# One kernel, three edits in its front: a stated engine order up to the first width transform, folds in three steps a group, and one-hot rows four chunks at a time

## The chip, the cores and the metric

The kernel runs on one core of a Trainium2 chip. The metric is device time in microseconds, the median of several executions. A core has TensorE (PE; its weight loads are PEld), VectorE (DVE), ScalarE (ACT), GpSimd (POOL), and SyncE (SP), which here only issues DMAs. Each engine has its own queue of instructions; semaphores order the engines among each other.

## The reference

Three steps, of float32 arrays; x is 8 x 3072 x 256:

```python
X = np.fft.fft(x, axis=1); X = np.fft.fft(X, axis=2); x = X.real.reshape(24576, 256)
# then, over the rows in order: 8 experts, capacity 768
expert = argmax(x @ w_gate); gate = softmax(x @ w_gate)[expert]
# the first 768 rows of each expert are kept; all other rows of the output are zero
y = relu(x_kept @ w1[e]) @ w2[e]              # 256 -> 1024 -> 256
out = gate * y
# then for every row
h = out @ w_in; out = maximum(0.01 * h, h) @ w_out   # 256 -> 2048 -> 256
```

Since at most 8 x 768 rows are not zero, the kernel transforms only the batches in which the experts fill up: two whole ones and half of a third (NSTAT = 3), and checks at the end that they were enough.

## The kernel before

Everything that needs float32 precision on TensorE is split into a high and a low part (`split`: ACT copies the high part, VectorE subtracts it from the source, which gives the low part, the residue), and a product is three matmuls (`mm3`, lines 199 to 201: high x low parts of both sides).

For each batch the work has four stages.

- **Fold** (`fold_steps`): x comes in three chunks of 128 x 8 x 256 (`xj`, 1 MB, two buffers, loaded by SP in `next_x`). VectorE folds the eight symmetric rows and two halves of columns into sums and differences: `a0` makes `fe` (sums), differences in place, and `q` (differences of differences, also in place, in the second half of x); `a1` works on `fe`, `b0` on `q`; both write `raw`. `a0` ends with the load of the next chunk. A stated list gives the order of the nine steps.
- **S1**, the transform over the sequence: `raw` is split to `fh` and `fl` (`fsplit_j`, for batch 0 by chunk; `fsplit_steps` for the others, by pairs of classes), and multiplied by the tables `th`, `tl`. Batch 0 runs S1 chunk by chunk (`s1_first`: all eight accumulators stay open, and `group(j)` adds chunk j); the others run class by class (`s1_steps`). The accumulators are evacuated to `pch`, `pcl`, `psh`, `psl` by ACT and VectorE (`s1_ev_odd`, `s1_ev_even`).
- **S2**, the transform over the width, with the gate's eight columns beside it (`s2_steps`): 12 chunks of 128 rows, 14 matmuls each in batches 0 and 1 (7 in batch 2), into `psu`; ACT evacuates to `yd`, `ym`, sends them to memory and copies the logits to L. The matmul of line 643 adds the special rows: `spec` times the small table `smov`.
- **Routing** (`route`): `one`, `mm`, `two` find each row's expert and place; then `put`: for each of 25 chunks, `hot` builds two one-hot rows on VectorE (`oha`, `ohr`: lines 819 and 820) and `place` multiplies them on TensorE, which writes row numbers into the slot table (`tab`, `self.slots`). From the table `prep` (GpSimd) gathers the experts' rows.

Ahead of batch 0's S2 stand also: the tables, loaded in six halves through staging tiles that share the room of `pch` to `psl` (`load_table`); the width tables `mv..` (`build_tables`); the gate's columns and `smov` (`build_gate`); the column of x that has no partner (`special_fold`, `special`, whose result is `spec`).

After the routing of two batches the experts start (`moe_static`), TensorE-heavy, with the other weights' conversion as background; then the last two products.

What sets the order: the program emits instructions in one order; a scheduler reorders them by its own model of time, on all engines but SP, which keeps the emission order (`in_order("SP")`, line 1443). Background steps wait in a list `bg` with a cost each; `step` emits a foreground step, adds its credit, and emits background steps as far as the credit goes; `upto` empties the list. Lines 1196 to 1241 emit the front.

Of the kernel before, what the change touches and what calls it, by code (L numbers as in the profile page):

```python
# [8 lines left out]
F32 = mybir.dt.float32  # L9
# [134 lines left out]
class Kern:  # L144
# [91 lines left out]
    def build_tables(self, tmp, yp, nb):  # L236
# [11 lines left out]
        nc.sync.dma_start(out=sk, in_=a[f"sk{nb}"])  # L248
        self.sk = sm, sk

    def build_gate(self, tmp, nb):
        nc = self.nc
        f, ft, wg = self.b0[:3]
        mv = self.smov[nb]
        sm, sk = self.sk
        ps = self.ps2.tile([P, 512], F32, name="ps_c", tag="v")
        for i in range(2):
            for k in range(2):
                nc.tensor.matmul(out=ps[:, 8 * i:8 * i + 8], lhsT=ft[:, k, 128 * i:128 * i + 128],
                                 rhs=wg[:, k], start=k == 0, stop=k == 1)  # L260
        for k in range(2):
            nc.tensor.matmul(out=ps[:96, 16:24], lhsT=ft[:, k, 256:352], rhs=wg[:, k],
                             start=k == 0, stop=k == 1)
        for i, n in enumerate("csn"):
            hi, lo = self.mv[n + "h"], self.mv[n + "l"]
            if n == "n":
                self.act(hi[:, D:], self.mv["sh"][:, D:].bitcast(F32), scale=-1.0)
                self.act(lo[:, D:], self.mv["sl"][:, D:].bitcast(F32), scale=-1.0)
            else:
                self.split(hi[:, D:], lo[:, D:], ps[:, 8 * i:8 * i + 8])  # L270
        wh = tmp.tile([96, E], F32R, name="wh", tag="wh")
        wl = tmp.tile([96, E], F32R, name="wl", tag="wl")
        self.split(wh, wl, ps[:96, 16:24])
        self.act(mv[:, :, :D], sm)
        V = nc.vector
        for b in range(nb):
            t0 = tmp.tile([96, E], F32, name="smt0", tag="smt0")
            V.tensor_scalar(out=t0, in0=wh.bitcast(F32), scalar1=sk[:, b, 0:1], scalar2=None, op0=ALU.mult)
            t1 = tmp.tile([96, E], F32, name="smt1", tag="smt1")
            V.tensor_scalar(out=t1, in0=wl.bitcast(F32), scalar1=sk[:, b, 1:2], scalar2=None, op0=ALU.mult)  # L280
            self.tt(mv[:, b, D:], t0, t1, ALU.add)
# [47 lines left out]
    def fold_steps(self, b):  # L329


        tmp = self.tmp

        def copy(o, x):
            self.nc.vector.tensor_copy(out=o, in_=x)
        st, loc, xt, kb = [], {}, self.xt, bkey(b)
        tt = self.tt
        A, M = ALU.add, ALU.subtract

        def extra():  # L340
            xe = xt[kb, "e"]
            t = tmp.tile([1, 3 * P], F32, name="ee", tag="ee")
            c7, x4, o7 = (t[:, P * i:P * i + P] for i in range(3))
            tt(t[:, :D], xe[:, 0], xe[:, 1], A)
            tt(xe[:, 0], xe[:, 0], xe[:, 1], M)
            tt(c7, c7, x4, A)
            tt(o7, xe[:, 0, :P], xe[:, 0, P:], M)
            loc["c7"], loc["o7"], loc["x4"] = c7, o7, x4

        def fix():  # L350
            ce, r, c7 = loc["ce", 0], loc["r"], loc["c7"]
            tt(r[0:1, 4, 0], ce[0:1, 0], c7, M)
            tt(r[0:1, 5, 0], ce[0:1, 0], c7, A)
            copy(loc["x4"], ce[0:1, 1])

        def a0(j):
            x = xt[kb, j]
            if j == 0:
                extra()
            if j == 0:  # L360
                loc["r"] = self.rawp.tile([P, 8, 3, P], F32, name="raw", tag="raw")
            e = tmp.tile([P, 8, P], F32, name="fe", tag="fe")
            q = x[:, 0:4, P:]
            loc["e"], loc["o", j] = e, q
            tt(e, x[:, :, :P], x[:, :, P:], A)
            tt(x[:, :, :P], x[:, :, :P], x[:, :, P:], M)
            tt(q, x[:, 0::2, :P], x[:, 1::2, :P], M)
            self.next_x()

        def a1(j):  # L370
            e, r = loc["e"], loc["r"]
            c = e[:, 0::2]
            tt(c, c, e[:, 1::2], A)
            ce = tmp.tile([P, 2, P], F32, name="ce", tag="ce")
            loc["ce", j] = ce
            tt(ce, c[:, 0::2], c[:, 1::2], A)
            tt(r[:, 0:2, j], c[:, 0::2], c[:, 1::2], M)
            tt(r[:, 4, j], ce[:, 0], ce[:, 1], M)
            tt(r[:, 5, j], ce[:, 0], ce[:, 1], A)
            if j == 0:  # L380
                fix()

        def b0(j):
            o, r = loc["o", j], loc["r"]
            se = tmp.tile([P, 2, P], F32, name="se", tag="se")
            tt(se, o[:, 0::2], o[:, 1::2], M)
            tt(r[:, 2:4, j], o[:, 2::-2], o[:, 3::-2], A)
            tt(r[:, 6, j], se[:, 0], se[:, 1], A)
            tt(r[:, 7, j], se[:, 0], se[:, 1], M)
            if j == 0:  # L390
                copy(r[0:1, 3, 0], r[0:1, 2, 0])
                copy(r[0:1, 6, 0], se[0:1, 1])
                copy(r[0:1, 2, 0], loc["o7"])

        ca = (3.1, 2.1, 1.6)
        for f, j in ((a0, 0), (a1, 0), (a0, 1), (b0, 0), (a1, 1), (a0, 2), (b0, 1), (a1, 2), (b0, 2)):
            st.append((ca[(a0, a1, b0).index(f)], lambda f=f, j=j: f(j)))
        self.floc = loc
        return st
# [112 lines left out]
    def s1_first(self):  # L512
# [7 lines left out]
        def group(j):  # L520
            for fn, cls in (("c", 0), ("s", 2)):
                for par in "AB":
                    js = [jj for jj, _, _ in self.ODD[par]]
                    if j in js:
                        self.s1_mm(banks[fn + par][:, :384], cls, "A", j, j == js[0], j == js[-1], par)
            for cls, name, fn, r, n in self.EVEN:
                w = 386 if name == "C" else 384
                self.s1_mm(banks[name][:, :w], cls, name, j, j == 0, j == 2 and name != "C")
                if j == 2 and name == "C":
                    self.s1_extra(banks[name][:, :w])  # L530

        def evens(q):
            for e in self.EVEN[q:q + 2]:
# [88 lines left out]
    def s2_steps(self, b, L, bi, mode):  # L622
# [29 lines left out]
        for c in range(12):  # L652
# [6 lines left out]
            def go(c=c, m=m):  # L659
# [10 lines left out]
                if m == "v":  # L670
                    V = self.ps2.tile([P, 512], F32, name="psv", tag="v")
                    part(V[:, :NL], "s", "s", c, True, True)
                    vs = yp.tile([P, NL], F32, name="vs", tag="vs", bufs=1)
                    self.act(vs, V[:, :NL])
                    self.tt(yd, U[:, :NL], vs, ALU.subtract)
                    self.tt(ym, U[:, :NL], vs, ALU.add)
# [18 lines left out]
        if mirror:  # L695
            def mid():
                U = cosp("p", 12, True, 1)
                y = yp.tile([1, NR], F32, name="yx", tag="vs", bufs=1)
                self.act(y[:, :NL], U[:1, :NL])
                self.act(y[:, NL:], rt[0:1, 1, 12:13])  # L700
                nc.scalar.dma_start(out=dst(1536 + 3, 1), in_=y)
# [7 lines left out]
    def route(self, b, L, n):  # L709
# [2 lines left out]
        V, G = nc.vector, nc.gpsimd  # L712
        loc = {}
        nput = min(n, NCH - 1)

        def t3(name, dt=F32):
            return rp.tile([P, NCH, E], dt, name=name, tag=name)[:, :n]
# [89 lines left out]
                    self.act(o, t)  # L807
                loc.update(hi=hi, lo=lo)

        w = self.ntab // P  # L810
        w2 = w + w % 2

        def hot(c, m):

            a = rp.tile([P, HG, P], F32, name="oha", tag="oha", bufs=2)
            r = rp.tile([P, HG, w2], F32, name="ohr", tag="ohr", bufs=2)
            for i in range(m):
                k = slice(c + i, c + i + 1)
                V.tensor_scalar(out=a[:, i], in0=self.iota, scalar1=loc["lo"][:, k], scalar2=None, op0=ALU.is_equal)
                V.tensor_scalar(out=r[:, i], in0=self.iota[:, :w2], scalar1=loc["hi"][:, k],  # L820
                                scalar2=self.rt[:, b, 0, k], op0=ALU.is_equal, op1=ALU.mult)
            loc["h", c] = a, r

        def place(c, m):
# [338 lines left out]
    def static(self, rps):  # L1163
# [28 lines left out]
        def run(*steps):  # L1192
            for f in steps:
                f[1]() if isinstance(f, tuple) else f()

        run(fs[0], fs[1], fs[3], *tb[0])
        tb.append(self.load_table(self.pt, 2))
        self.special_load(0)
        self.load_consts()
        self.reset_routing()  # L1200
        self.load_build(self.tmp, self.yp)
        run(lambda: ready(0), fs[2], fs[4], *tb[1], fs[6], lambda: ready(1), fs[5], fs[7], fs[8], *tb[2],
            lambda: self.build_tables(self.tmp, self.yp, NSTAT), lambda: ready(2))
        self.special_fold()
        self.later(self.fold_steps(1))
        loc = self.floc
        self.new_p()
        ev = [f for _, f in evac]
        run(ev[0], ev[1], lambda: self.build_gate(self.tmp, NSTAT), ev[2], ev[3], self.special)
        pend, put0 = None, []  # L1210
        for b in range(NSTAT):
            last = b == NSTAT - 1
            if b:
# [13 lines left out]
                    self.later(fs[:1] + [(1.5, mm), (1.5, two)] + fs[1:])  # L1227
                for s in self.s1_steps():
                    self.step(*s)
            if not last:  # L1230
                self.later(self.fsplit_steps(loc))
                if b:
                    self.later(put)
            L = self.new_l()
            for s in self.s2_steps(b, L, b, (lambda c: "d") if last else
                                   (lambda c: "p")):
                self.step(*s)
            self.upto(len(put) if b and not last else 0)
            if last:
                self.full_flag()  # L1240
            pend = self.route(b, L, 12 if last else NCH)
# [109 lines left out]
    def general(self):  # L1351
        tc, nc = self.tc, self.nc
        with ExitStack() as es:
# [6 lines left out]
                    fn()  # L1360
            self.load_build(self.tmp, self.yp)
            self.build_tables(self.tmp, self.yp, 1)
            self.build_gate(self.tmp, 1)
            self.init_table()
            if not self.fast:
# [129 lines left out]
```

## Time and profile before

| | |
|---|---|
| median of 3 runs | 1030.39 us (1030.28 to 1030.99) |
| profiled execution | 1030.87 us, its span 1029.1 us |
| busy in the span | PE 951.8 (92%), PEld 903.2 (88%), DVE 636.4 (62%), ACT 481.8 (47%), POOL 126.8 (12%) |
| mean granted clock of TensorE | 0.974 of full speed |

The shares are means over the whole span; stages differ, and the rows below go by stretches.

### The profile page before, as it was taken

Reading aid. Unit: us, or ns where it says so; the run is one execution under the profiler, and the core shown is the slowest. Engines: PE = TensorE matmul, PEld = TensorE weight load, DVE = VectorE, ACT = ScalarE, POOL = GpSimd, SP = SyncE. Lnnn points to the kernel's source line nnn. Section 1 sums busy time; section 2 is a strip of 40 time slices with the busy share of each in tenths; the row PEclk is TensorE's granted clock in tenths of the full one; section 3 lists DMA queues with packets and bytes.
Section 4 is the critical chain, followed back from the end, with each engine's and each line's share of the span. In section 5 each row is a group of like instructions: output and inputs, shape, how many; then the busy total and the mean of one; then the engine's idle time right before and its main releaser. Section 6 shows DMA issues by size and latency. Waiting matters only on the chain. (4 is left out here: it accounts for less than half of the span.)

```text
span 1029.1 us, 15401 instructions
## 1 busy us (share of the span) xinstructions
PE 951.8 (92%) x5563; PEld 903.2 (88%) x5563; DVE 636.4 (62%) x1445; ACT 481.8 (47%) x1075; POOL 126.8 (12%) x178
## 2 busy tenths in 40 slices
PE   1749997989999999999999999999999999999993
PEld 1639996888999999998999999999999999999992
DVE  8997575979898635453555555555455555555551
ACT  4234631546665534453544444444444454445441
POOL 1000002063232221100001100110011100110011
PEclk9969997999999999999999999999999999999997
DMA  8324522479879655400000000000010000000000
GB/s 312 129 87 164 190 83 75 156 232 322 302 264 366 207 190 193 144 32 31 20 28 32 16 22 26 32 22 21 21 32 32 16 17 32 33 16 6 11 16 18
DMA packets 56192, 101.51 MB, mean 99 GB/s; under 512 B 5189, under 2 KB 39369, under 8 KB 54956
## 3 DMA queue, kind: packets, MB, share of 16 engines
q1 hardware_dynamic: 47000, 73.20, 21.1%
q0 software_dynamic: 4640, 12.81, 3.8%
q10 hardware_dynamic: 4468, 14.44, 3.5%
q8 instruction: 45, 0.74, 0.3%
q14 instruction: 39, 0.32, 0.1%
HBM read 54.54 MB, written 45.89 MB: 98 GB/s over the span
## 5 line engine op out<-in xcount | busy, mean ns | idle before, releaser
L185 DVE TENSOR_TENSOR gf<-gt,psg 128x384 f32<-128x384 f32 x256 | 141.8, 554 | 218.2 <-ACT gt L188 214.8
L188 ACT ACTIVATE gt<-psg 128x384 f32<-128x384 f32 x256 | 126.0, 492 | 253.7 <-PE psg L201 253.6
L1099 PE MATMUL po<-wo,gh 128*128 128x512 f32 x768 | 232.3, 394 | 0.0
L199 PE MATMUL psg<-yh,wi 128*128 128x384 f32 x512 | 172.7, 338 | 1.9 <-ACT yh L188 1.9
L200 PE MATMUL psg<-yl,wi 128*128 128x384 f32 x512 | 173.0, 338 | 0.0
L201 PE MATMUL psg<-yh,wi 128*128 128x384 f32 x512 | 172.7, 337 | 0.0
L185 DVE TENSOR_TENSOR gl<-gf,gh 128x384 fp32r<-128x384 f32 x256 | 141.4, 552 | 17.5 <-ACT gh L188 17.4
L1099 PEld LDWEIGHTS po<-wo,gh 128*128 128x128 f32 x768 | 139.8, 188 | 12.3
L1100 PE MATMUL po<-wo,gl 128*128 128x256 f32 x768 | 149.6, 281 | 0.0
L188 ACT ACTIVATE gh<-gf 128x384 fp32r<-128x384 f32 x256 | 132.8, 519 | 18.1 <-PE po L1099 17.8
L1100 PEld LDWEIGHTS po<-wo,gl 128*128 128x128 f32 x768 | 128.4, 188 | 4.0
L1110 POOL DMA_INDIRECT out<-ob,mix x48 | 46.9, 977 | 551.5 <-DVE ob L1109 477.9
L1042 DVE SCALAR_TENSOR_TENSOR hl<-psh,hh 128x384 fp32r<-128x384 f32 x128 | 70.0, 553 | 60.8 <-ACT hh L188 60.2
L199 PEld LDWEIGHTS psg<-yh,wi 128*128 128x128 f32 x512 | 96.6, 189 | 9.4 <-ACT yh L188 2.2
L200 PEld LDWEIGHTS psg<-yl,wi 128*128 128x128 f32 x512 | 96.8, 189 | 8.3
L201 PEld LDWEIGHTS psg<-yh,wi 128*128 128x128 f32 x512 | 96.5, 188 | 2.1
L199 PE MATMUL psy<-hh,w2h 128*128 128x384 f32 x256 | 87.9, 343 | 0.8 <-DVE hl L1042 0.8
L199 PE MATMUL psh<-xTh,w1h 128*128 128x384 f32 x256 | 86.8, 340 | 1.9 <-DVE hl L1042 1.3
L201 PE MATMUL psy<-hh,w2l 128*128 128x384 f32 x256 | 86.4, 338 | 0.0
L200 PE MATMUL psy<-hl,w2h 128*128 128x384 f32 x256 | 86.2, 337 | 0.0
L201 PE MATMUL psh<-xTh,w1l 128*128 128x384 f32 x256 | 86.0, 336 | 0.0
L200 PE MATMUL psh<-xTl,w1h 128*128 128x384 f32 x256 | 85.9, 336 | 0.0
(224 smaller groups left out, 1421.9 us busy)
## 6 DMA issues: line engine op xcount, KB each, us to landing
out<-zero SPq DMA_DIRECT2D x48, 512.0 KB, 8.8
xj<-in_xg SPq DMA_DIRECT2D x9, 1024.0 KB, 5.0
w1r<-in_w SPq DMA_DIRECT2D x9, 1024.0 KB, 7.9
w2r<-in_w SPq DMA_DIRECT2D x9, 1024.0 KB, 7.2
y_kept<-yf ACTq DMA_DIRECT2D x16, 384.0 KB, 6.2
yf<-y_kept SPq DMA_DIRECT2D x16, 384.0 KB, 3.0
y_first<-yd ACTq DMA_DIRECT2D x9, 530.0 KB, 2.8
w<-in_w_in SPq DMA_DIRECT2D x8, 512.0 KB, 5.2
```

What stands on the lines that cost most here:

```text
L185: self.nc.vector.tensor_tensor(out=o, in0=x, in1=y, op=op)
L188: self.nc.scalar.activation(out=o, in_=x, func=func, scale=scale)
L199: nc.tensor.matmul(out=out, lhsT=lh, rhs=rh, start=start and i == 0, stop=False)
L200: nc.tensor.matmul(out=out, lhsT=lh, rhs=rl, start=False, stop=False)
L201: nc.tensor.matmul(out=out, lhsT=ll, rhs=rh, start=False, stop=stop and i == n - 1)
L1042: nc.vector.scalar_tensor_tensor(out=lo, in0=ps[:, :T], scalar=0.0, in1=hi.bitcast(F32), op0=ALU.max, op1=ALU.subtract)
L1099: mm(out=o, lhsT=gh[:, c], rhs=both, start=f == 0, stop=False)
L1100: mm(out=o[:, :D], lhsT=gl[:, c], rhs=first, start=False, stop=f == NF2 - 1)
L1110: i = nc.gpsimd.indirect_dma_start(out=self.a["out"][0:nr], out_offset=bass.IndirectOffsetOnAxis(ap=s["ix"][:, k, 1:2], axis=0), in_=ob, i ...
```

## The change

1. The engine order of PE, DVE, ACT and POOL is stated (emission order) from the fold of batch 0 to the end of its S2; behind that point the scheduler orders again. The front's emission is rewritten: fold steps, table halves, `ready(j)`, `build_tables`, `special_fold`, `build_smov` (moved out of `build_gate`), evacuations, `build_gate`, `special`; batch 1's fold and fsplit become background steps beneath S2 of batch 0 (before, its fold was put in the list earlier, and fsplit after it). In `group(j)` the cosine classes, odd and even, go ahead of the sine classes. In `build_gate` the three copies go ahead of the three subtractions.
2. `q` gets a tile of its own (`fq`), so b0 no longer reads x; each chunk's steps go a0, a1, b0. `vs` and `yx` take tiles of the ring `ev`.
3. `hot` makes the one-hot rows of up to four chunks with three operations instead of two for each chunk.

```diff
+    def build_smov(self, nb):
+        self.act(self.smov[nb][:, :, :D], self.sk[0])
...
-        for i, n in enumerate("csn"):
-            hi, lo = self.mv[n + "h"], self.mv[n + "l"]
-            if n == "n":
-                self.act(hi[:, D:], self.mv["sh"][:, D:].bitcast(F32), scale=-1.0)
-                self.act(lo[:, D:], self.mv["sl"][:, D:].bitcast(F32), scale=-1.0)
-            else:
-                self.split(hi[:, D:], lo[:, D:], ps[:, 8 * i:8 * i + 8])
...
-        self.split(wh, wl, ps[:96, 16:24])
-        self.act(mv[:, :, :D], sm)
+        parts = [(self.mv["ch"][:, D:], self.mv["cl"][:, D:], ps[:, :8]),
+                 (self.mv["sh"][:, D:], self.mv["sl"][:, D:], ps[:, 8:16]), (wh, wl, ps[:96, 16:24])]
+        for hi, _, src in parts:
+            self.act(hi, src)
+        for hi, lo, src in parts:
+            self.tt(lo, src, hi, ALU.subtract)
+        for h in "hl":
+            self.act(self.mv["n" + h][:, D:], self.mv["s" + h][:, D:].bitcast(F32), scale=-1.0)
...
-            q = x[:, 0:4, P:]
+            q = tmp.tile([P, 4, P], F32, name="fq", tag="fq")
...
-        for f, j in ((a0, 0), (a1, 0), (a0, 1), (b0, 0), (a1, 1), (a0, 2), (b0, 1), (a1, 2), (b0, 2)):
+        for f, j in ((a0, 0), (a1, 0), (b0, 0), (a0, 1), (a1, 1), (b0, 1), (a0, 2), (a1, 2), (b0, 2)):
...
-            for cls, name, fn, r, n in self.EVEN:
-                w = 386 if name == "C" else 384
-                self.s1_mm(banks[name][:, :w], cls, name, j, j == 0, j == 2 and name != "C")
-                if j == 2 and name == "C":
-                    self.s1_extra(banks[name][:, :w])
+                for cls, name, _, r, n in [e for e in self.EVEN if e[2] == fn]:
+                    w = 386 if name == "C" else 384
+                    self.s1_mm(banks[name][:, :w], cls, name, j, j == 0, j == 2 and name != "C")
+                    if j == 2 and name == "C":
+                        self.s1_extra(banks[name][:, :w])
...
-                    vs = yp.tile([P, NL], F32, name="vs", tag="vs", bufs=1)
+                    vs = yp.tile([P, NL], F32, name="vs", tag="ev", bufs=3)
...
-                y = yp.tile([1, NR], F32, name="yx", tag="vs", bufs=1)
+                y = yp.tile([1, NR], F32, name="yx", tag="ev", bufs=3)
...
-            for i in range(m):
-                k = slice(c + i, c + i + 1)
-                V.tensor_scalar(out=a[:, i], in0=self.iota, scalar1=loc["lo"][:, k], scalar2=None, op0=ALU.is_equal)
-                V.tensor_scalar(out=r[:, i], in0=self.iota[:, :w2], scalar1=loc["hi"][:, k],
-                                scalar2=self.rt[:, b, 0, k], op0=ALU.is_equal, op1=ALU.mult)
+            o = rp.tile([P, HG, w2], F32, name="oho", tag="oho")
+            cs = slice(c, c + m)
+            at = lambda x, k: x[:, cs, None].to_broadcast([P, m, k])
+            row = lambda k: self.iota[:, None, :k].to_broadcast([P, m, k])
+            self.tt(a[:, :m], at(loc["lo"], P), row(P), ALU.is_equal)
+            self.tt(o[:, :m], at(loc["hi"], w2), row(w2), ALU.is_equal)
+            self.tt(r[:, :m], o[:, :m], at(self.rt[:, b, 0], w2), ALU.mult)
...
-        run(fs[0], fs[1], fs[3], *tb[0])
+        front = self.in_order("PE", "DVE", "Activation", "Pool")
+        front.__enter__()
+        run(fs[0], tb[0][0], fs[1], fs[2], tb[0][1])
         tb.append(self.load_table(self.pt, 2))
         self.special_load(0)
         self.load_consts()
         self.reset_routing()
         self.load_build(self.tmp, self.yp)
-        run(lambda: ready(0), fs[2], fs[4], *tb[1], fs[6], lambda: ready(1), fs[5], fs[7], fs[8], *tb[2],
-            lambda: self.build_tables(self.tmp, self.yp, NSTAT), lambda: ready(2))
+        run(lambda: ready(0), fs[3], tb[1][0], fs[4], fs[5], tb[1][1], lambda: ready(1))
+        self.build_tables(self.tmp, self.yp, NSTAT)
         self.special_fold()
-        self.later(self.fold_steps(1))
-        loc = self.floc
+        run(tb[2][0], fs[6], tb[2][1], fs[7], fs[8], lambda: ready(2))
+        self.build_smov(NSTAT)
         self.new_p()
         ev = [f for _, f in evac]
         run(ev[0], ev[1], lambda: self.build_gate(self.tmp, NSTAT), ev[2], ev[3], self.special)
+        fs, loc = self.fold_steps(1), self.floc
+        split = self.fsplit_steps(loc)
+        self.later(fs[:2] + split[:1] + fs[2:] + split[1:])
...
-            if not last:
-                self.later(self.fsplit_steps(loc))
-                if b:
-                    self.later(put)
+            if b and not last:
+                self.later(self.fsplit_steps(loc) + put)
...
             self.upto(len(put) if b and not last else 0)
+            if not b:
+                front.__exit__(None, None, None)
```

## Rows read from the trace of the kernel before

**Rows 1.** Busy time by stretch: bounds, length, engines (instructions), granted clock, DMA share, GB/s

```profile
52.40:67.90 15.50, 0.45 (x3) 0.19 (x2) 15.28 (x40) 5.80 (x13) 0.00 (x0) 0.63 0.25 76
67.90:92.00 24.10, 24.10 (x175) 23.95 (x176) 21.10 (x53) 11.58 (x37) 0.00 (x0) 0.88 0.46 178
92.00:129.20 37.20, 37.20 (x264) 35.27 (x263) 21.55 (x67) 20.30 (x60) 0.33 (x3) 1.00 0.45 163
...
220.00:1015.00 795.00, 786.02 (x4511) 748.27 (x4509) 463.99 (x934) 392.48 (x855) 99.89 (x118) 1.00 0.25 86
```

**Rows 2.** Waits of TensorE in the first 240 us: total, times, longest

```profile
PE psu L643 <- ACT fh L188: 15.1, 1, 15.1
```

**Rows 3.** Timeline of TensorE: start, length, instruction, what ended its idle time

```profile
52.43 0.41 PE L617 MATMUL ps<-altn,th 1*96 1x386 f32 x1
67.90 0.56 PE L643 MATMUL psu<-smov,spec 96*128 96x264 f32 x1 [15.05 <-ACT fh L188]
...
91.61 0.34 PE L199 MATMUL ps<-th,fh 128*128 128x384 f32 x1
...
128.62 0.33 PE L199 MATMUL ps<-th,fh 128*128 128x384 f32 x1
```

**Rows 4.** Timeline of VectorE: the first chunk, and the end of the hole

```profile
5.94 1.23 DVE L185 TENSOR_TENSOR fe<-xj 128x1024 f32<-128x1024 f32 x1 [2.54 <-DMA xj<-in_xg]
...
64.33 1.02 DVE L185 TENSOR_TENSOR spec<-tx,spec 32x384 fp32r<-32x384 f32 x2
...
66.46 1.22 DVE L185 TENSOR_TENSOR fe<-xj 128x1024 f32<-128x1024 f32 x1
67.60 0.15 DVE L185 TENSOR_TENSOR smov<-smt,smt 96x8 fp32r<-96x8 f32 x1
```

**Rows 5.** VectorE's groups by shape up to 176 us: count, busy, mean ns, idle before

```profile
L185 DVE TENSOR_TENSOR fe<-xj 128x1024 f32<-128x1024 f32 x9 | 10.9, 1211 | 2.5 <-DMA xj<-in_xg 2.5
...
L185 DVE TENSOR_TENSOR tl<-tst,th 128x1153 fp32r<-128x1153 f32 x6 | 8.1, 1346 | 0.0
L185 DVE TENSOR_TENSOR fl<-raw,fh 128x768 fp32r<-128x768 f32 x8 | 7.3, 948 | 0.1
L185 DVE TENSOR_TENSOR fe<-fe 128x512 f32<-128x512 f32 x9 | 6.1, 676 | 0.0
...
L185 DVE TENSOR_TENSOR t<-ps,tb 128x384 f32<-128x384 f32 x9 | 4.7, 549 | 2.0 <-ACT tb L188 2.0
L185 DVE TENSOR_TENSOR raw<-ce 128x128 f32<-128x128 f32 x18 | 4.3, 277 | 0.0
...
L185 DVE TENSOR_TENSOR se<-xj 128x256 f32<-128x256 f32 x9 | 3.7, 412 | 0.1
```

**Rows 6.** Timeline of VectorE: one-hot rows, and 512 columns in two forms

```profile
157.00 0.28 DVE L819 TENSOR_SCALAR oha<-iota,slotl 128x128 f32<-128x128 f32 x1
157.20 0.30 DVE L820 TENSOR_SCALAR ohr<-iota,sloth,rt 128x48 f32<-128x48 f32 x1
157.41 0.28 DVE L819 TENSOR_SCALAR oha<-iota,slotl 128x128 f32<-128x128 f32 x1
...
196.80 0.42 DVE L900 TENSOR_SCALAR r<-w 128x512 uint32<-128x512 uint32 x1
197.14 0.68 DVE L185 TENSOR_TENSOR w1l<-w1r,w1h 128x512 fp32r<-128x512 f32 x1
197.74 0.42 DVE L900 TENSOR_SCALAR r<-w 128x512 uint32<-128x512 uint32 x1
```

**Rows 7.** Timeline behind the last S2: place matmuls, slot table, first transposes

```profile
161.17 6.83 PE L830 MATMUL pst<-ohr,oha 128*128 128x48 f32 x36
...
168.03 0.20 DVE L185 TENSOR_TENSOR tab<-tab,pst 128x48 f32<-128x48 f32 x1
...
173.21 0.66 PE L1023 MATMUL pst<-ident,xg 128*128 128x128 f32 x2 [5.21 <-issue]
```

**Rows 8.** Timeline of SP's queue and of ACT: a chunk's load, an fh copy

```profile
12.28 0.33 SPq L326 DMA_DIRECT2D xj<-in_xg  x1
...
69.06 0.85 ACT L188 ACTIVATE fh<-raw 128x768 fp32r<-128x768 f32 x1 [1.30 <-DVE raw L185]
```

More of the change, by code (lines that the diff above doesn't have):

```diff
@@ L714, in route @@
         nput = min(n, NCH - 1)
+        w = self.ntab // P
         def t3(name, dt=F32):
@@ L808, in two @@
                 loc.update(hi=hi, lo=lo)
-        w = self.ntab // P
         w2 = w + w % 2
@@ L1209, in static @@
         run(ev[0], ev[1], lambda: self.build_gate(self.tmp, NSTAT), ev[2], ev[3], self.special)
-        pend, put0 = None, []
+        fs, loc = self.fold_steps(1), self.floc
+        split = self.fsplit_steps(loc)
+        self.later(fs[:2] + split[:1] + fs[2:] + split[1:])
+        pend = None
         for b in range(NSTAT):
@@ L1362, in general @@
             self.build_tables(self.tmp, self.yp, 1)
+            self.build_smov(1)
             self.build_gate(self.tmp, 1)
```

## The prediction

> **What bounds the kernel now.** I read the busy times by stretch first [rows 1]. From 220 us to 1015 us TensorE works 786.02 of 795 us at a granted clock of 1.00: nothing in this change touches that stretch, and it can only start sooner or later as a whole. The holes are ahead of it. The list of what TensorE waited for [rows 2] names the largest one after the start: 15.1 us before the first width matmul of batch 0 (psu, line 643). On TensorE's own timeline [rows 3] the hole runs from 52.43 to 67.90, and the first such matmul takes 0.56 us, because the clock has fallen: the stretch behind it has a mean of 0.88. From 67.90 to 129.2 there is no other hole [rows 1]. The list puts the wait down to an ACT copy; VectorE's timeline shows what was really late [rows 4]. The transform needs the special rows (spec) and the small table smov; their last pieces come at 64.33 and 67.60, and between them VectorE works on folds, by 66.46 on batch 2's (of nine fe of 1024 columns [rows 5], three a batch, this is the seventh). VectorE is busy 15.28 of these 15.5 us, but with work not yet wanted, while from 92.0 to 129.2 it is busy only 21.55 of 37.2. So up to 67.9 the order on VectorE sets the time; then TensorE does; and at the end the one-hot rows do: the slot table is updated at 168.03, while the width transform's last matmuls were issued at 161 [rows 7].
>
> **Costs used.** Successive independent tensor_tensor operations overlap by some 0.07 us: the 128x512 one that starts at 197.14 takes 0.68, and the next starts at 197.74 [rows 6]. So each duration of rows 5 counts less 0.07. One fold chunk is two operations of 1024 columns (2 x 1.14), two of 512 (2 x 0.61), four of 256 (4 x 0.34), four of 128 (4 x 0.21): 5.7; three chunks are 17.1, and with eleven one-partition operations of 0.13 to 0.3 some 19.2 a batch.
>
> **Part 1, the stated order of the front.** It removes the choice by which batch 1's and 2's folds ran ahead of batch 0's tables. On VectorE, from the arrival of x at 5.94 [rows 4] to the last special row, what must run is: fold of batch 0, 18.1 (its first four small operations need only xe, and precede x); six table residues, 6 x 1.28 = 7.7; three residues fl of 1024 columns, 3.4; the width tables, 1.2; the special fold, 2; twelve evacuation operations of 384 columns, 12 x 0.48 = 5.8; the gate's twelve small ones, 1.8 (estimated from the 0.15 of smov [rows 4]); the special's six of 384 columns, 2.9. Sum 42.9, hence 48.8 with no stall. A stated order adds stalls, since what waits holds all behind it. I count 0.9 before the third table's first half (ACT copies it only after the special fold's copies), 1.9 for the first odd pair of matmuls of group 2, 2.6 for the sine group and the twelve gate matmuls, some 1.8 for ACT round trips: 7.2. So spec is complete at 56 instead of some 65, smov well before it, and S2 of batch 0 starts at 56, 11.9 sooner. Bounds: 48.8 (no stall) and 63.2 (twice these stalls). I take 56.
>
> S2 of batch 0 took 67.90 to 91.61, 23.7 us at a mean clock of 0.88 [rows 1, 3]; at full clock that is 21. TensorE now pauses some 2.5 us ahead of it instead of 15, and I take full clock (if it falls all the same, 2.7 more): end at 77.2. Fold 1 runs on VectorE beneath it: 56 + 19.2, and 1 us for the copy xh, which stands on ACT behind four steps' evacuations: 76.2, hidden by 1 us. If S2's cover were gone it would cost all 19. The four fh copies (0.85 each [rows 8]) stand on ACT behind all evacuations and result DMAs of S2, and the fl's behind them; the third matmul needs the first fl. So S1 of batch 1 starts, effectively, at 79.2: 77.2 + 0.85 + 0.95 + handovers of some 0.5, less the two matmuls that need no fl. Before: 91.61. **Gain so far 12.4.**
>
> **Part 2, folds that free x early, and the DMA queue.** The third difference goes to a tile of its own, so x is free after three operations instead of behind b0: the next x load is issued at about 9 instead of 12.28 [rows 8], and later loads likewise. No wait on x stands on the critical path then; I price it at 0, at most 2 where a chunk would have been late. The other way, the second half of the first table is split only behind b0 of chunk 0, at 15.3; SP's load of the third table's second half waits for that staging buffer, and the special's inputs, constants, routing table, mcs, mcsT, gate weights, tri and the next batch's x wait behind it on the same queue, some 2.5 us longer. The first needed is mcs, wanted at 25; 0, at most 1. The yx row that now shares a ring of three with tb, t1 and t3 costs 0: its DMA is done before the third is written.
>
> **Part 3, batch 2's fold, moved.** It ran from 66.46 to 89, beneath S2 of batch 0; that place now belongs to fold 1. Its 19.2 us must go beneath S1 and S2 of batch 1, which take TensorE 37.0 us (91.61 to 128.62 [rows 3]). VectorE had 21.55 there. Of that, four w1 residues (2.4), two groups of one-hot rows (3.3) and three of four fl (2.6) may go later: 13.2 remain. Add 19.2 and the four fl of batch 1 (3.5): 35.9 of 37. It just fits; waits of VectorE on ACT and on TensorE make it late by 0 to 6. I take 1.
>
> **Part 4, one-hot rows, four chunks at a time.** A chunk's pair takes 0.41 (157.00 to 157.41 [rows 6]), a group of four 1.64. Now: one compare of 4 x 128 columns, 0.61; one of 4 x 48, whose length lies between 128 and 256 columns, 0.34, in full since the product waits for it; the product 0.27 and some 0.03: 1.25. Less 0.39 a group, 13 full groups up to 168: 5. Bounds, as no row has both operands broadcast in this form: 0.9 (all overlapped) and 2 (the elements at twice the price).
>
> By the rows, the tensor_scalar form is the faster one per column: 128x512 takes 0.34 so (196.80 to 197.14) and 0.60 as tensor_tensor; but at 128 columns both take 0.28 with 0.21 to the next [rows 5, 6]: there the fixed share rules, and four chunks in one instruction pay it once. The Trainium skill, VectorE: DVE Perf Modes, Mode 2x_2P, has the rule that speaks against this edit: float32 tensor_scalar makes two results a cycle, float32 tensor_tensor one. By that rule alone, an estimate, a group would take twice as long, 3.3, the tail would lose 7 (a third of 13 x 1.66) and the sum below be -4.4; the trace agrees on the rates, but by its rows the group takes 1.25.
>
> From S1 of batch 2 to the slot table were 39.4 us (128.62 to 168.03). VectorE gets 2.6 + 2.4 + 2.5 more there (what part 3 put off) and about 5 less; its waits on place matmuls shrink as it falls behind. The last seconds, after S2, are one-hot groups back to back, about 3 to 5 of them: 1.5 less. I take 1.5 less overall (bounds: 1.5 more, 4 less). Behind it prep, the gathers and the transposes at 173.21 [rows 7] follow with their old distance.
>
> **Sum.** -12.4 + 1.0 - 1.5 = -12.9 against the profiled execution: span 1029.1 to 1016.2, its time 1030.87 to 1018.0. That execution is 0.5 above the median 1030.39; from the median the forecast is 1017.5.
>
> **The rivals.**
> 1. VectorE becomes the bound under batch 1. For it: 35.9 of 37. Then S1 of batch 2 is 6 instead of 1 late and the one-hot tail gives nothing: -12.4 + 6 = -6.4, 1024. Against it: fold pieces are short and have no waits but their own.
> 2. The other side: the stated order stalls VectorE. One place: ACT stands at mvch or the special fold's copies for a late load, all later table copies stand behind it, and VectorE behind them. It decides when stalls reach 19.1 us (67.9 - 48.8) instead of 7.2. At 23 us S2 starts 4 late, the full clock gives 2.7 back, and fold 2 beneath batch 1 costs 2: 3 slower, 1033.5. Against it: the loads that matter are issued 2.5 us later, not 16.
> 3. The start is sooner, but the gain is hidden: the stretch behind 220 waits for weights or gathers instead. Then 2 or less remains, 1029. Against it: DMA share 0.25 there and 9 us of idle TensorE in 795 [rows 1].
> 4. The one-hot groups lose their gain: the lower rate of tensor_tensor, and operands repeated over columns, which no row shows at this size, make a group 2. Then 13 groups cost 13 x 0.36 = 4.7 more, of which the tail has a third, 1.5: -12.4 + 1 + 1.5 = -9.9, 1020.5. For it: the rates of rows 6. Against it: 0.61 for 512 columns is a measured price.
>
> **How the numbers follow.** Forecast 0.55 (1014 to 1020), rival 4 0.10, rival 1 0.20, rival 3 0.06, rival 2 0.09. Within 0.2% (2.1 us) is what a measurement here cannot tell from no change; rival 3 lies there mostly. Faster 0.86, same 0.05, slower 0.09. The range goes from 1012 (stalls of 4 and the tail's lower bound: -12.4 - 3.2 + 1 - 4 = -18.6) to 1026 (rival 1 with 2 more); rivals 2 and 3 are left out.
>
> **What would show it.** Right: first psu matmul near 56 (52 to 60), no fold of batch 1 before the last spec, the first S1 matmul of batch 1 at 78 to 80 with the clock at 1.00 since 57, S1 of batch 2 at 116 to 118, one-hot groups of 1.25 us, the slot table near 154. Wrong: a psu start past 62, a hole between S2 and the next S1 of more than 4 us, or a transform of batch 2 that waits for fh.

## The result, and the profile after

The changed kernel takes 1039.74 us (median of 4, 1039.24 to 1043.31), the kernel before 1030.34 on the same chip: ratio 1.0100, 95% interval 1.0082 to 1.0118. It is slower by 1.0%; the forecast was 1017.5 and faster, its range 1012 to 1026. The profiled execution spans 1041.4 us, 12.3 more than before, at a granted clock of 0.961.

TensorE's timeline of the changed kernel has the places where the stages begin: S2 of batch 0, a stop in it, S1 of batch 1, a stop in that, S1 of batch 2, the first transposes.

```profile
60.48 0.59 PE L645 MATMUL psu<-smov,spec 96*128 96x264 f32 x1 [4.84 <-DVE spec L185]
...
87.40 0.59 PE L645 MATMUL psu<-smov,spec 96*128 96x264 f32 x1 [2.69 <-ACT ym L188]
...
91.17 0.69 PE L199 MATMUL ps<-th,fh 128*128 128x384 f32 x1 [3.19 <-ACT fh L188]
...
111.61 0.19 PE L758 MATMUL psr<-rs,tri 128*128 128x32 bf16 x1 [3.91 <-DVE rs L751]
...
139.13 0.34 PE L199 MATMUL ps<-th,fh 128*128 128x384 f32 x1
...
182.89 0.66 PE L1027 MATMUL pst<-ident,xg 128*128 128x128 f32 x2 [5.00 <-issue]
```

Against [rows 3, 7] the difference of the spans falls into five legs, each beside what the forecast gave it:

| leg | before | after | difference | forecast |
|---|---|---|---|---|
| up to S2 of batch 0 | 67.90 | 60.48 | -7.4 | -11.9 |
| from there to S1 of batch 1 | 23.7 | 30.7 | +7.0 | -0.5 |
| S1 and S2 of batch 1 | 37.0 | 48.0 | +11.0 | +1.0 |
| S1 of batch 2 to the first transposes | 44.6 | 43.8 | -0.8 | -1.5 |
| from there to the end | 855.9 | 858.5 | +2.6 | 0 |

The hole that the change aimed at did shrink, from 15.05 us [rows 3] to 4.84. What it gave was gone by 91.17, where S1 of batch 1 starts only 0.4 sooner, and the next leg loses 11. (That the change costs the 2.6 us of the last leg is not shown: this execution is the longest of the four, and the other three, which span 1037.4 to 1038.1, left no trace. The leg differs 20 to 30 us behind the first transposes: there TensorE worked 6.05 of the 10 us at a granted clock of 0.66, before 9.54 at 1.00.)

Where VectorE's time went is seen in the busy times by stretch (PE, PEld, DVE, ACT, POOL, then granted clock, DMA share, GB/s), first of the kernel before:

```profile
5.90:60.00 54.10, 25.15 (x127) 21.52 (x127) 53.87 (x121) 20.00 (x39) 0.00 (x0) 0.94 0.57 205
60.00:90.00 30.00, 22.10 (x159) 22.13 (x160) 28.94 (x72) 13.56 (x37) 0.00 (x0) 0.77 0.39 143
90.00:125.00 35.00, 35.00 (x247) 33.07 (x246) 21.55 (x67) 18.34 (x51) 0.33 (x3) 1.00 0.37 129
```

and of the changed one:

```profile
5.90:60.00 54.10, 33.19 (x127) 27.55 (x127) 42.88 (x97) 19.84 (x37) 0.00 (x0) 0.80 0.45 166
60.00:90.00 30.00, 24.81 (x176) 24.15 (x176) 22.09 (x51) 11.55 (x41) 0.00 (x0) 0.84 0.56 194
90.00:125.00 35.00, 29.30 (x143) 25.44 (x144) 34.31 (x94) 12.77 (x29) 1.19 (x3) 0.80 0.13 48
```

Read the third busy column. Before, VectorE was idle for 1.3 us in all up to 90, and had 13 us to spare behind. Now it does 11.0 us less up to 60 and 6.9 less up to 90, and in the third stretch it is full: 34.31 of 35, while TensorE, which had worked all 35, works 29.30 at a clock of 0.80. What is late is the routing of batch 0 between the pieces of batch 2's fold. VectorE's timeline of the changed kernel, the two pauses that matter and then the routing's first and last operation with the folds' first pieces:

```profile
51.08 0.17 DVE L185 TENSOR_TENSOR mvcl<-ps_c,mvch 128x8 fp32r<-128x8 f32 x1 [4.26 <-ACT wh L188]
...
72.76 0.28 DVE L185 TENSOR_TENSOR xh<-ee,xh 1x128 fp32r<-1x128 f32 x1 [5.59 <-ACT xh L188]
...
86.73 1.22 DVE L185 TENSOR_TENSOR fe<-xj 128x1024 f32<-128x1024 f32 x1
...
90.49 0.37 DVE L736 TENSOR_REDUCE mx<-L 128x26 f32<-128x208 f32 x1 [2.53 <-ACT L L188]
...
99.72 1.20 DVE L185 TENSOR_TENSOR fe<-xj 128x1024 f32<-128x1024 f32 x1
...
110.25 1.21 DVE L185 TENSOR_TENSOR fe<-xj 128x1024 f32<-128x1024 f32 x1
111.39 0.17 DVE L751 CAST rs<-rs4f 128x56 bf16<-128x56 f32 x1
```

From mx to rs the routing takes 21 us. Before, the same eleven operations took 4.1, by VectorE's timeline of the kernel before:

```profile
93.15 0.37 DVE L733 TENSOR_REDUCE mx<-L 128x26 f32<-128x208 f32 x1 [4.16 <-ACT L L188]
...
97.27 0.18 DVE L748 CAST rs<-rs4f 128x56 bf16<-128x56 f32 x1
```

TensorE needs rs for the matmul of line 758 (into the tile psr), which stands inside S1 of batch 1 in its queue, so it stops there for 3.91 us and comes back at the low clock level (0.50 from 112 to 116, a mean of 0.65 from 112 to 119.8).

ACT's timeline of the changed kernel shows why VectorE and TensorE stood between 60 and 91:

```profile
72.43 0.29 ACT L188 ACTIVATE xh<-ee 1x128 fp32r<-1x128 f32 x1
...
86.58 0.21 ACT L188 ACTIVATE ym<-rt 128x4 f32<-128x4 f32 x1 [3.51 <-DMA y_first<-ym]
...
90.29 3.03 ACT L188 ACTIVATE fh<-raw 128x768 fp32r<-128x768 f32 x4
```

The one-row copy xh, for which VectorE waits 5.59 us, stands behind evacuations and the result DMAs that ACT itself issues. Ahead of 86.58 ACT waits 3.51 us for a result DMA, with 12 more instructions of S2 behind it, and the four fh copies with which S1 begins come last of all. (The DMA share is 0.99 from 80 to 84 us, with a load of x issued at 78.30; before, ACT's waits for result DMAs in this S2 were 0.45 to 0.79 us. That the load held up the result DMA was not tested.) What TensorE waits for in these two places, the result tile and fh, are its 2.69 and 3.19 us.

The one-hot rows, which took 1.64 us for four chunks [rows 6], are as forecast. VectorE's groups by shape in the changed kernel:

```profile
L185 DVE TENSOR_TENSOR oha<-slotl,iota 128x512 f32<-128x512 f32 x12 | 8.2, 686 | 5.6 <-PE pst L834 5.6
L185 DVE TENSOR_TENSOR oho<-sloth,iota 128x192 f32<-128x192 f32 x12 | 4.2, 354 | 0.2
L185 DVE TENSOR_TENSOR ohr<-oho,rt 128x192 f32<-128x192 f32 x12 | 4.2, 352 | 0.1
```

On the timeline a group goes from the ohr of 159.10 to that of 160.37: 1.27 us.

### The profile page after: what moved, and what is told of

It reads as the page before. It is cut to its first block, busy times and chain, and to the rows that moved or that the text cites. A ratio compares the mean times of both kernels' runs of the same rounds, so it can differ in the third digit from the quotient of the medians.

```text
span 1041.4 us, 15325 instructions
## 1 busy us (share of the span) xinstructions
PE 967.8 (93%) x5563; PEld 915.0 (88%) x5563; DVE 630.8 (61%) x1372; ACT 480.3 (46%) x1075; POOL 130.3 (13%) x178
## 5 line engine op out<-in xcount | busy, mean ns | idle before, releaser
L1103 PEld LDWEIGHTS po<-wo,gh 128*128 128x128 f32 x768 | 139.7, 188 | 12.3
L188 ACT ACTIVATE hh<-psh 128x384 fp32r<-128x384 f32 x128 | 62.3, 492 | 52.2 <-PE psh L201 50.4
```

The costliest lines, as they stand in the source:

```text
L188: self.nc.scalar.activation(out=o, in_=x, func=func, scale=scale)
L1103: mm(out=o, lhsT=gh[:, c], rhs=both, start=f == 0, stop=False)
```

## The experiments

The theory: the stated order is the whole loss. VectorE is the scarce engine up to 125 us; in a stated order each operation that waits holds all behind it; the 18 us that stay unfilled come back beneath batch 1 and stretch the routing there. Rivals: the new fold order and its loads, or the new one-hot rows, cost the time; or the price is another engine's order (ACT's queue) alone.

**e1: the order not stated, all else as changed.**

```diff
-        front = self.in_order("PE", "DVE", "Activation", "Pool")
-        front.__enter__()
...
-            if not b:
-                front.__exit__(None, None, None)
```

> The changed kernel without the stated order (all else as changed). Theory A (the stated order is what costs: batch 1's copies xh and fh wait on ACT behind S2's evacuations, so fold 1 ends late, and fold 2, which may not fill VectorE's pauses in the front, falls beneath batch 1, where VectorE becomes the bound): the scheduler again runs folds ahead, S1 of batch 1 lasts some 17 us instead of 28.7, time 1025 to 1031. Theory B (the rewritten emission, with batch 1's fold late in it, costs by itself): 1036 or more. Theory C (the new fold steps or the one-hot form cost): 1036 or more.

Measured: 1026.04 us against 1030.06, ratio 0.9965 (0.9952 to 0.9977). So the two statements that open and close the stated order cost 13.7 us (1039.74 to 1026.04), and without them the rest of the change is a gain. VectorE's column in e1's busy times by stretch is full again where it was before, and TensorE again works all 35 us of the third:

```profile
5.90:60.00 54.10, 28.29 (x127) 22.53 (x127) 53.92 (x124) 20.07 (x38) 0.00 (x0) 0.88 0.56 205
60.00:90.00 30.00, 27.80 (x197) 27.17 (x198) 29.41 (x72) 15.27 (x45) 0.14 (x2) 0.87 0.48 180
90.00:125.00 35.00, 35.00 (x249) 33.22 (x249) 20.13 (x57) 18.71 (x54) 0.19 (x1) 1.00 0.41 142
```

S2 of batch 0 starts at 62.20 here, later than with the stated order, and still S1 of batch 1 starts at 85.81 and S1 of batch 2 at 123.12.

**e2 and e3: the other two parts alone, on the kernel before.** e2 takes the three operations of `hot`; e3 the tile fq, the step order a0, a1, b0 and the ring.

```diff
# e2
+            self.tt(a[:, :m], at(loc["lo"], P), row(P), ALU.is_equal)
+            self.tt(o[:, :m], at(loc["hi"], w2), row(w2), ALU.is_equal)
+            self.tt(r[:, :m], o[:, :m], at(self.rt[:, b, 0], w2), ALU.mult)
# e3
-            q = x[:, 0:4, P:]
+            q = tmp.tile([P, 4, P], F32, name="fq", tag="fq")
```

> The kernel before with the one-hot rows four chunks at a time, nothing else. Theories A and B: a group takes some 1.3 us instead of 1.64, the slot table comes 1 to 3 us sooner, time 1026 to 1030. Theory C: 1033 or more.

> The kernel before with the fold's new tile and step order and the shared ring, nothing else. Theories A and B: within 2 us of before, 1028 to 1032, as no wait on x stands on the critical path. Theory C: 1033 or more.

Measured: e2 1030.83, ratio 1.0010 (0.9997 to 1.0024); e3 1029.80, ratio 0.9998 (0.9987 to 1.0009). Neither costs anything that can be measured, and neither gains. In e2's profile the first transposes stand at 170.41, 2.8 sooner than [rows 7] (1.6 of it behind the start of S1 of batch 2), and its span is 3.0 shorter; but that execution is the fastest of its ten, and the median shows no gain.

**e4: ACT left out of the stated order.**

```diff
-        front = self.in_order("PE", "DVE", "Activation", "Pool")
+        front = self.in_order("PE", "DVE", "Pool")
```

> The changed kernel with the order stated for PE, DVE and POOL, but not for ACT. Theory A, if ACT's queue is the place: xh no longer waits behind S2's evacuations (VectorE's stall of 5.6 us at 67.2 is gone), the fh copies go between evacuations, S1 of batch 1 starts at 84 to 87 instead of 91.2, and the time falls by 4 to 8 us, to 1032 to 1036. Theory A', that the order on VectorE is what keeps fold 2 late: fold 2 still lies beneath batch 1, and the time stays within 3 us of the changed kernel, 1037 to 1040.

Measured: 1041.45, ratio 1.0116 (1.0093 to 1.0138). ACT's share is real, S1 of batch 1 starts at 83.66, 7.5 sooner; but most of it is lost at the routing (S1 of batch 2 starts at 135.78, 3.4 sooner), and the median shows nothing of the rest. Both theories' times are missed, the second by 1.45. TensorE's timeline of e4:

```profile
107.54 0.18 PE L758 MATMUL psr<-rs,tri 128*128 128x32 bf16 x1 [11.00 <-DVE rs L751]
```

Freed of one wait, TensorE stands 11 us instead of 3.91 at the next. The rival that ACT's queue alone is the price falls.

**e5: the stated order ends ahead of S2 of batch 0.** Fold 1 and all of S2 are the scheduler's again.

```diff
         pend = None
+        front.__exit__(None, None, None)
         for b in range(NSTAT):
...
-            if not b:
-                front.__exit__(None, None, None)
```

> The changed kernel with the stated order ending ahead of S2 of batch 0 instead of behind it. If the order within S2 of batch 0 (fold 1 held behind the copy xh, the fh copies behind the evacuations) is what costs: VectorE runs fold 1 and then fold 2 without the pause at 67 to 73, S1 of batch 1 starts at 82 to 85, and the time falls to 1026 to 1033. If the loss comes from the routing matmuls that hold TensorE under batch 1 whenever fold 2 lies there: 1036 or more, with a wait of 4 us or more for rs.

Measured: 1049.95, ratio 1.0192 (1.0175 to 1.0209), the slowest of all. VectorE has no pause now (52.41 of the 54.1 us up to 60, 29.79 of the next 30), but what fills it is the wrong work: folds of batches 1 and 2 start at 56.30, 63.14, 74.19 and 85.02 between the small operations that make spec. TensorE's timeline of e5:

```profile
86.88 0.59 PE L645 MATMUL psu<-smov,spec 96*128 96x264 f32 x1 [26.13 <-DVE spec L185]
```

TensorE doesn't stop for rs in this run, so neither theory has its signs, though the time is that of the second. An idle VectorE is not the loss by itself; it is idle time and the order of what fills it.

**e6 and e7: the routing's matmul later.** e6 puts `mm` and `two` of batch 0 behind the fold of batch 2 in the list; e7 is e6 with e4's edit.

```diff
-                    self.later(fs[:1] + [(1.5, mm), (1.5, two)] + fs[1:])
+                    self.later(fs + [(1.5, mm), (1.5, two)])
```

> The changed kernel with the routing matmuls of batch 0 (mm, and two behind them) put behind fold 2 in the list of background steps, so that they stand later in TensorE's queue. If TensorE is held by its place in line (rs is late because fold pieces come between the small dependent operations of the routing): the wait for rs goes, S1 of batch 1 takes some 18 us instead of 28.7, and the time falls by 5 to 10 us, to 1030 to 1035. If VectorE's amount of work sets the end under batch 1: S1 of batch 2 starts no more than 3 us sooner, 1037 or more.

> Both: ACT's order not stated, and the routing matmuls of batch 0 behind fold 2. If the two delays add up: S1 of batch 1 starts at 84 and TensorE goes through it without the wait of 11 us, S1 of batch 2 starts at 118 to 124 instead of 135.8, time 1022 to 1030. If VectorE's amount of work is the bound: 1034 or more.

Measured: e6 1041.98, ratio 1.0115 (1.0086 to 1.0143); e7 1034.65, ratio 1.0050 (1.0034 to 1.0067). In e6 S1 of batch 2 starts at 130.6, 8.5 sooner than in the changed kernel (2.6 of it already at S1 of batch 1, ahead of which the edit changes nothing), and the transposes at 184.08, 1.2 later: TensorE stops at the same matmul, 5.6 us, one batch further on. In e7 S1 of batch 1 starts at 84.76 and that of batch 2 at 122.98, as in e1, but the stop at psr (4.5 us) is there too, and the transposes come at 174.86 against e1's 167.21. VectorE's late work had only been put off. Both times lie in the range of the second expectation, though in e6 S1 of batch 2 comes sooner than that allows.

**e8: batch 2's fold left out on VectorE** (GpSimd writes zeros for raw). With a third batch of zeros the experts' places don't fill, and the kernel ends in its general path: its total, 3216.39 us, can't be compared. Its trace up to batch 2 can.

```diff
         def a0(j):
+            if kb == 2:
+                if j == 0:
...
+                    self.nc.gpsimd.memset(loc["r"], 0.0)
...
+                self.next_x()
+                return
```

> The changed kernel without the fold of batch 2 on VectorE (left out: its 19 us of sums and differences; GpSimd writes zeros in their place, all loads and all later work stay). If fold 2 beneath batch 1 is what makes S1 of batch 1 last 28.7 us: 17 to 19 us there, S1 of batch 2 at 126 to 130 instead of 139, time 1027 to 1031. If S1 of batch 1 stays above 24 us, fold 2 is not it.

Measured: S1 of batch 1 starts where it did (91.54) but ends after 19.8 us instead of 28.7; S1 of batch 2 starts at 131.38 instead of 139.13. The same stretch of e8, and then of the changed kernel:

```profile
91.50:111.30 19.80, 19.76 (x93) 16.82 (x94) 15.41 (x43) 6.57 (x14) 3.00 (x4) 0.84 0.21 86
```

```profile
91.50:111.30 19.80, 15.58 (x68) 12.25 (x68) 19.77 (x48) 4.36 (x9) 0.14 (x2) 0.84 0.17 56
```

With the fold away VectorE has room (15.41 of 19.8), the routing takes 7.6 us instead of 21, and TensorE has no hole. So 8.9 of the 12 us by which S1 of batch 1 grew are the fold's (before it took 16.7); the other 3.1 are the clock, 0.84 instead of 1.00.

**e9 and e10: steps of batch 1's fold written into VectorE's pauses**; e10 with e4's edit too.

```diff
-        run(ev[0], ev[1], lambda: self.build_gate(self.tmp, NSTAT), ev[2], ev[3], self.special)
...
-        self.later(fs[:2] + split[:1] + fs[2:] + split[1:])
+        run(fs[0], ev[0], ev[1], fs[1], split[0], fs[2],
+            lambda: self.build_gate(self.tmp, NSTAT), ev[2], ev[3], self.special)
+        self.later(fs[3:] + split[1:])
```

> The changed kernel, order stated as there, with the first three fold steps of batch 1 and its xh, xl put by hand into VectorE's pauses in the front (the first ahead of the first evacuation, the others ahead of the gate). Theory P (what costs is that the stated order leaves VectorE idle: 11 us up to 60 and 7 more up to 90, and pushes as much fold work beneath batch 1): those idle times shrink by 10 or more together, S2 of batch 0 starts at 59 to 62, fold 2 ends by 105 instead of 117, S1 of batch 1 lasts 18 to 22 us instead of 28.7, time 1028 to 1034. Rival Q (TensorE's order and clock in the front, or ACT's queue, set it whatever VectorE does): 1037 or more.

> The same with ACT's order not stated. Theory P: the fh copies no longer wait for the end of S2's evacuations; S1 of batch 1 starts at 83 to 85, as without the filling, and now goes on without the wait of 11 us for rs; time 1022 to 1028. Rival Q: 1036 or more.

Measured: e9 1040.59, ratio 1.0104 (1.0085 to 1.0122); e10 1036.28, ratio 1.0063 (1.0045 to 1.0081). e9 fills 6.7 of the 11 us (VectorE works 49.62 up to 60), and S1 of batch 1 starts 4.8 sooner, at 86.33; but the time has nothing of it, for VectorE then stands here, by its timeline of e9:

```profile
85.00 1.83 DVE L185 TENSOR_TENSOR fl<-raw,fh 128x768 fp32r<-128x768 f32 x2 [5.40 <-ACT fh L188]
...
91.73 0.96 DVE L185 TENSOR_TENSOR fl<-raw,fh 128x768 fp32r<-128x768 f32 x1 [3.75 <-ACT fh L188]
```

raw has one buffer: batch 2's fold may not write it before batch 1's fl has read it, and fl waits for fh copies that stand behind S2 on ACT. The routing is late again, and TensorE stops for it longer than in the changed kernel, by its timeline of e9:

```profile
111.33 0.19 PE L758 MATMUL psr<-rs,tri 128*128 128x32 bf16 x1 [8.75 <-DVE rs L751]
```

With ACT free too (e10) VectorE's waits for fh go, S1 of batch 1 starts at 86.53, and TensorE's stops beneath batch 1 that are left are 1.9 us for pcl and 3.4 at psr. A second buffer of raw was not tried. Both times lie in rival Q's range, not in theory P's.

**e11: VectorE alone left out of the stated order.**

```diff
-        front = self.in_order("PE", "DVE", "Activation", "Pool")
+        front = self.in_order("PE", "Activation", "Pool")
```

> The changed kernel with the order stated for PE, ACT and POOL, but not for VectorE. Theory P, as far as idle time alone counts: VectorE is 95% busy up to 90 and the time falls to 1026 to 1033. Theory P with the reservation that the run with the order ended before S2 showed (a scheduler that fills every pause can put fold steps between the dependent operations of spec and hold S2): S2 of batch 0 starts after 70, and the time is 1036 or more although VectorE is never idle.

Measured: 1037.87, ratio 1.0078 (1.0060 to 1.0096). VectorE is busy up to 60 again (53.78 of 54.1), and then stands, by the list of its waits from 60 to 95 us:

```profile
DVE mx L736 <- ACT L L188: 12.5, 1, 12.5
DVE xh L185 <- ACT xh L188: 8.8, 1, 8.8
```

Its free order runs ahead into work that ACT, in its stated order, delivers late: S2 of batch 0 starts at 67.20 (not after 70, so only the time is as the second theory has it), and S1 of batch 1 at 94.29, 2.7 later than in the kernel before. But from there S1 and S2 of batch 1 take 37.2 us as before, not 48.0. VectorE is busy 33.77 of these 37.2, two of the three chunks of batch 2's fold lie in them, and still TensorE works through at a granted clock of 1.00: the routing takes 11.8 us, and rs comes just before TensorE's queue gets to psr. So fold work beneath batch 1 doesn't by itself cost the 11; it does when the routing comes too late for TensorE's queue.

**e12: three at once**: steps in the pauses (e9), ACT free (e4), the routing's matmul late (e6).

> The three suspected costs of the stated order taken away together: steps of batch 1's fold written into VectorE's pauses, ACT's order left to the scheduler, and the routing's matmul behind the fold of batch 2. Theory (the loss is VectorE's unfilled time, ACT's queue and the stop at psr, and these add): each of the three alone moved the wait to the next; together the first S1 matmul of batch 1 stands at 86 to 87 as with the first two, that of batch 2 at 123 to 126 as with the last two (37 to 39 us later), and the time comes to 1030 to 1033, ratio 1.000 to 1.003. Rival (an order that is stated has a cost of its own, since what the scheduler doesn't see of it is queued wrongly behind it): S1 of batch 2 at 123 too, but TensorE stops at psr beneath batch 2 for 4 us or more, low clock behind it, and the time stays at 1034 to 1037, ratio 1.004 to 1.007.

Measured: 1031.29, ratio 1.0021 (1.0009 to 1.0033), against 1.0100 with none of the three. S1 of batch 1 starts at 87.61, that of batch 2 at 125.58, the transposes at 169.61; TensorE's stop at psr is 1.3 us. Its busy time by stretch, the third stretch:

```profile
90.00:125.00 35.00, 34.77 (x244) 32.78 (x242) 24.31 (x63) 19.87 (x59) 0.71 (x3) 1.00 0.37 133
```

TensorE works through at full clock with VectorE at 24.31. Against the kernel before on the same chip, 9.4 us of loss have become 1.5 (1031.29 to 1029.78). The three costs together are nearly all of the loss against the kernel before, though each alone gave back nothing (e4, e6, e9) and the pairs that were run half (e7) or a third (e10). The rival's signs, a stop at psr of 4 us or more and a time of 1034 to 1037, are not there; but a further cost of the stated order stays possible, since e12 is still 5 to 6 us behind e1 (1031.29 against 1026.04, ratios 1.0021 and 0.9965). In the two profiles 2.4 us of this are there at the first transposes (169.61 against 167.21), and 3.1 come behind them, where TensorE's granted clock 20 to 30 us on is 0.66 in e12 and 0.83 in e1.

## Why the prediction was wrong

- **The hole.** Right in place, off in size: 60.48, not 56, inside the bounds 48.8 to 63.2. Stalls of VectorE came to 11.6 us (60.48 less 48.8) rather than 7.2. Up to the third fl (39.91, 1.12 us of wait ahead of it) they were small; then the gate's matmuls and evacuations came late, the largest pause being the 4.26 before mvcl, where TensorE worked 7.75 of 8 us from 40 to 48 at a granted clock of 0.50. The forecast's 2.6 for this place names no clock. e6 shows what it is worth: its front's code is the same, TensorE was granted 0.69 from 40 to 48, the pause was 2.67, and S2 started at 58.64.
- **"Gain so far 12.4".** This step failed: 0.4 was left. S2 did not run at full clock (0.50 from 60 to 64, 0.83 over the leg); the wait for xh was 5.59 us, not 1; ACT stood 3.51 us for a result DMA, for which I had no term; and the fh copies came behind all of it. Of the leg's 30.7 us TensorE worked 24.8 instead of 21 and stood 5.9 (2.69 and 3.19) instead of some 2. The wait for xh is not among these, since the first fh copy waited for ACT, not for VectorE; what it did was to move fold 2 later. I had named ACT's queue and priced it as four steps' evacuations of their own length, without the waits in them. e4 shows the term: free of the order, ACT lets S1 of batch 1 start 7.5 us sooner. (The sum also ends S2 at 77.2, where 56 + 21 is 77.0; that decides nothing.)
- **Part 3, "35.9 of 37. It just fits".** This step failed, and is the larger: S1 and S2 of batch 1 took 48.0. The sum of the work is not what was wrong: VectorE worked 39.49 us of the leg's 48.0, and e11 put 33.77 into 37.2 without loss. What the step left out is the delay of small operations that depend on each other between long ones: VectorE, full from 90 to 125 us (34.31 of 35), makes the routing last 17 us longer in the middle, and TensorE, in order, stops for it (3.91) and loses its clock. e8 gives the price of the moved fold: 8.9 us. That is near rival 1, which had VectorE as the bound under batch 1, at some 11 us instead of 6, but with another mechanism: a late chain, more than too much work.
- **Rival 2**, the only one on the slower side, was sought at one place with a threshold of 19.1 us of stalls before S2. The stalls there stayed at 11.6; the slower side came from behind the start of S2, where I had priced no stall of the stated order beyond the 1 us for xh.
- **The signs.** None of the three signs of being wrong was seen: the psu start was 60.48, the hole ahead of S1 of batch 1 was 3.19, and S1 of batch 2 waited for nothing. The signs of being right caught it: the first S1 matmul came at 91.17 instead of 78 to 80, S1 of batch 2 at 139.13 instead of 116 to 118.
- **Part 2.** Right: the load of x is issued at 9.23 (about 9 forecast) instead of 12.28 [rows 8], and e3 measures the part at nothing.
- **Part 4.** Right in the price, 1.27 us a group for 1.25, with both operands repeated over columns. Rival 4's 2 us falls. The rates of the Trainium skill, VectorE: DVE Perf Modes, Mode 2x_2P, taken as the only price, gave an estimate of 3.3, and the trace does not bear that out. The 1.5 us that it should give showed as 0.8 in the changed kernel's profile, as 1.6 in e2's, and as none in e2's median.
- **Open:** why e1 is 4.0 us faster than before, when e2 and e3 give nothing alone (the rewritten emission, as the scheduler takes it, or all of it together); and what keeps e12 behind e1. TensorE alone left out of the stated order, and VectorE's pauses filled together with the late matmul, were not run.

The version to keep is e1: the folds, the one-hot groups and the new emission, with the order left to the scheduler: 1026.04 us, 0.35% (0.23 to 0.48) faster than before.

## What to carry to other kernels

Before fixing an engine's order, add up the idle time that the free order fills, and ask where that work goes when it is displaced: the scarce engine pays it back later, and a stretch that "just fits" on paper can delay the chains of small operations in it many times over (from 4.1 us to 21 here, to 11.8 in e11, where nothing had to wait for them). Price a queue by the waits of what stands ahead, DMAs included, not by its busy time. And undo such costs together before judging any one of them: three edits that each measured nothing were together worth 8 of 9.4 us.

## What the runs showed of the hardware that was not expected

TensorE's clock fell in the front although its work began sooner. These are the changed kernel's stretches from 24 to 36 and 40 to 48 us:

```profile
24.00:36.00 12.00, 10.38 (x36) 8.27 (x36) 10.60 (x22) 4.89 (x9) 0.00 (x0) 0.57 0.39 123
40.00:48.00 8.00, 7.75 (x21) 6.37 (x22) 4.21 (x7) 2.96 (x6) 0.00 (x0) 0.50 0.00 0
```

A granted clock of 0.50 is the lower level, 1.2 GHz. The kernel before was granted 1.00 over the first of these stretches, with TensorE busy 8.74 of the 12 us (for the first matmuls of either kernel the view's 1.00 doesn't hold: those of 384 columns took 0.52 us each, here up to 21.3, before up to 25.4, and then 0.33 or 0.34). Here TensorE had started at 15.43 instead of 20.74 and stood for 2.05 us ahead of 25.31, and around that pause the clock fell: up to 34.9 the matmuls took 0.52 again. Before, it stood 2.24 us ahead of 29.75 and kept the full clock, 0.34 a matmul. So the earlier start doesn't settle it either: in e1 TensorE started at 20.75, as before, stood 1.84 us ahead of 29.76, and its granted clock was 0.50 from 30.5. The same length of pause thus went both ways, and no run here settles why.
